# A weight-gradient stage that lands its loads in the place of WoT, starts them one step early, and walks its tiles downwards

## The chip, the cores and the metric

The kernel runs on one core of a Trainium2 chip. The metric is device time in microseconds (us); three runs of the kernel before gave 4724.1 to 4726.25, median 4724.49. One further execution was taken by the hardware profiler; every line of a profile below is from such an execution.

A core has five engines with their own instruction queues: PE (TensorE, matrix products; its weight loads are shown apart as PEld), DVE (VectorE), ACT (ScalarE), POOL (GpSimd) and SP (SyncE, which here only issues transfers). Transfers (DMAs) are issued on SP's, ACT's and POOL's queues.

## The reference

It is the backward pass of a block with a recurrent attention layer and a gated MLP, for 2048 tokens of width 640. The attention goes through the tokens in 64 segments of 32. Eight memory rows go ahead of each segment, and the first eight output rows are the memory of the next:

```
for s in range(n_seg):
    h = concatenate([mem, xs])              # 8 + 32 rows
    q, k, v = h @ Wq, h @ Wk, h @ Wv        # 32 heads of 128
    p = softmax(where(mask, q k^T * scale, -1e9))
    o = (p v) @ Wo
    mem = o[:8]; outs.append(o[8:])
```

The block returns `x + s * g`, where `s` is the attention of the normalised `x` and `g` a gated MLP of it. Asked for are the output and the gradients with respect to x, mem0, Wq, Wk, Wv, Wo, w1, w2 and w3, for a given `grad_out`. This document is about the point where the recurrence of the backward pass has ended and the gradients of Wq, Wk and Wv begin.

## The kernel before

The kernel goes through stages: MLP forward with the normalisation, the recurrence forward, the recurrence backward (`phase4_Abwd`), the gradients of the attention's projections (`phase6_Awgrads`), the gradient of Wo (`phase6b_gWo`) and the MLP backward (`phase5_Bbwd_ln`). In each of the stages of interest `in_order` fixes the instructions of each engine to the order in which the code writes them. Between two stages a scheduler may interleave, as long as buffers and data allow it. It also sets the semaphores: an instruction waits for whatever last used its buffer. A buffer is a range of the on-chip memory (SBUF); pools are stacked, and a later pool lies where an earlier one has been.

**The loop ahead.** `phase4_Abwd` runs `chain(t, gap)` for t from 63 down to 0 (L1184). Each step is one chain of dependent small products: the memory gradient times WoT (`packed_half`, L306), the gradients of v, k and q for eight rows, and the products of these with WvT, WkT and WqT (`packed_out`, L325), which `fold_add` sums into `fsum`. The next step needs that sum. In between, `gap` calls other work at named points (W0, W1, G1 to G6); in the last steps there is none left to call. The step's outputs go to device memory (HBM): rows of `GOS`, `DSR`, and, after the last step, the stores `out_dram<-fsum` by `fold_store`. The WoT matrix fills the tile tagged `w0` and WqT the one tagged `w1` of pool W0, 40 KB per partition each.

**The gradient stage.** The tokens are cut into 22 tiles (`NTL`): 20 of three segments with 96 tokens and 24 memory rows, then one with 96 and 24 and one with 32 and 8. The heads are cut into 8 quarters of four heads (the code calls a quarter `qd`). A unit is a pair of quarter and tile; 176 units are worked through, quarter by quarter, in the tile order 20, 21, 0, 1, ..., 19. For a unit,

- `ld(u)` (L1542) loads `dS` and `P` (120 x 512) and three row tiles `r` (g, q, k). SP issues five transfers and POOL three to six small ones for the memory rows (`load_m`, L245). There are five sets of buffers (`NB`).
- `s1` (L1563) transposes `dS` on PE, and DVE copies the result to `dST`.
- `s2` (L1573) forms three products (PE, L1578), which ACT and DVE copy out as gradient rows (`gr`, or `grs` for tiles 20 and 21, L1585 to L1589).
- `s3` (L1602) transposes these (PE, L1610), and ACT and DVE copy them into a ring (`ghacc`, at L92 and L90), which holds the last 384 tokens and a fixed piece of 128.
- `s4` (L1623) takes a block of 128 tokens from the ring, multiplies it by the quarter's weights `w` in twelve matmuls (L1628), and adds to `ghacc`, the running sum of the input gradient. The list `parts` says at which position in the quarter each half block is due.
- `wg` (L1642), at a quarter's end, multiplies the token rows `hr` by all gradient rows `gr` to give 512 columns of each weight gradient (PE, L1647).

The stage begins with `ld_to(3)`, `ld_w(0)` (three weights of 640 KB), `ld_to(5)` and `head(0)`, that is s1, s2 and s3 of the first two units. Then the loop at position p of a quarter loads unit p + 7, multiplies unit p + 2, transposes unit p + 3, turns unit p + 1 and does the s4 due. At units 6 to 11 SP also loads `hr`, 3.3 MB in all. The memory for all this is taken when pool W0 is already closed: first the sum and ring (pool `xw`), which lie where WoT and WqT were, and above them the stage's own buffers.

**Semaphores of transfers.** SP's transfers take eight semaphores in turn, POOL's another eight. A transfer waits for the one eight places before on its queue to have landed.

Of the kernel before, what the change touches and what calls it, by code (L numbers as in the profile page):

```python
# [9 lines left out]
BF16 = mybir.dt.bfloat16  # L10
# [6 lines left out]
P = 128  # L17
# [250 lines left out]
def turned_load(k, dst, src):  # L268

    k.nc.sync.dma_start_transpose(dst, src)  # L270
# [118 lines left out]
def phase3_Afwd(k, W0, W4, Wv, Wk_, out2):  # L389
    nc, tc = k.nc, k.tc  # L390
    D, DC, S, H, HD, T = k.D, k.DC, k.S, k.H, k.HD, k.T
    Wq = W4.tile([P, DC, HD], BF16, name="Wq", tag="w2")
    Wo = W4.tile([P, H, D], BF16, name="Wo", tag="w3")
    with tc.tile_pool(name="ast", bufs=1) as st:
        kTs = [st.tile([P, H, 120], BF16, name=f"kT{i}") for i in range(2)]

        vt = st.tile([P, HD // 2], BF16, name="vt")
        hxs = [st.tile([P, DC, 32], BF16, name=f"hx{i}") for i in range(2)]
        qTs = [st.tile([P, 4, P], BF16, name=f"xqT{i}") for i in range(3)]
        xPs = [st.tile([P, 4, P], BF16, name=f"xP{i}") for i in range(3)]  # L400
        PTs = [st.tile([P, 4, P], BF16, name=f"xPT{i}") for i in range(2)]
        oTm = st.tile([P, H, 32], BF16, name="oTm")
        first_part(k, Wv, Wk_, Wq, Wo, kTs, vt, hxs, qTs + xPs + PTs + [oTm])
        with tc.tile_pool(name="aps", bufs=1, space=bass.MemoryType.PSUM) as ps, \
                tc.tile_pool(name="apm", bufs=1, space=bass.MemoryType.PSUM) as psm:
            banks = [psm.tile([P, 512], F32, name=f"bank{i}") for i in range(3)]
            own = kTs, vt, hxs, qTs, xPs, PTs, oTm
            WT = recurrence(k, W0, W4, Wv, Wk_, Wq, Wo, own, ps, banks)
            phase4_Abwd(k, out2, W4, WT, own, ps, banks)


def first_part(k, Wv, Wk_, Wq, Wo, kTs, vt, hxs, rest):
# [667 lines left out]
        eng.dma_start(k.GX0[x0 - k.GB0:x0 - k.GB0 + w, cg * 1024:(cg + 1) * 1024], sg[0:w, :])  # L1080


def phase4_Abwd(k, out2, W4, WT, own, ps, banks):
    nc, tc = k.nc, k.tc
    D, DC, S, H, HD, T = k.D, k.DC, k.S, k.H, k.HD, k.T
    out2f = out2.flatten_outer_dims()
# [4 lines left out]
    for s in range(3):  # L1091
        t0 = (2, 0, 1)[s]
        n = (T - 1 - t0 + 2) // 3
# [10 lines left out]
    with tc.tile_pool(name="gst", bufs=1) as st, tc.tile_pool(name="gchain", bufs=1) as ch, \  # L1104
# [6 lines left out]
        four = lambda ap: ap.rearrange("p (i c) -> p i c", i=4)  # L1111
# [281 lines left out]
        def gap_of(t):  # L1393
            def at(f, tt, i0, i1=None):
                b = batch.get(tt, ())
                for u in b[i0:i0 + 1 if i1 is None else i1]:
                    f(*u)

            def gap(g):
                if g == "W0":  # L1400
                    ride_ld(t - 1)
                    at(turn, t, 0)
                elif g == "W1":
                    at(turn, t, 1)
                    at(gmem_ld, t + 1, 2)
                elif g == "G1":
                    at(dprob, t, 0)
                elif g == "G2":
                    at(dprob, t, 1)
                    at(turn, t, 2)  # L1410
                    at(dsoft, t, 0)
                elif g == "G3":
                    if t > 0:
                        load_xp(t - 1)
                    at(dsoft, t, 1)
                    at(gmem_ld, t, 0)
                elif g == "G4":
                    at(dprob, t, 2)
                elif g == "G5":
                    at(gmem_ld, t, 1)  # L1420
                elif g == "G6":
                    at(dsoft, t, 2)
                for i in range(WARM.get(g, 0)):
                    nc.tensor.matmul((bA if g in ("W1", "G2") else bB)[:], k.ident[:], WqT[:, 0, 0:512], start=True, stop=True)
            return gap
        todo = pro + todo

        def chain_consts():
            nc.gpsimd.memset(bdf, 0.0)
# [61 lines left out]
                nc.gpsimd.dma_start(*later.pop(0))  # L1491
        assert not later
        in_order(k, start)


def phase6_Awgrads(k, X, out0, out3, out4, out5):

    nc, tc = k.nc, k.tc
    D, DC, S, H, HD, T, NTL, NT = k.D, k.DC, k.S, k.H, k.HD, k.T, k.NTL, k.NT
# [5 lines left out]
    R = 384  # L1505
    NB = 5
    assert NS == 8 * NF and NW == NF and (96 * NF) % R == 0 and S - 96 * NF == P
    order = [NF, NF + 1] + list(range(NF))
    with tc.tile_pool(name="h6i", bufs=3) as io, tc.tile_pool(name="h6", bufs=1) as hp, \
            tc.tile_pool(name="h6g", bufs=1) as gp, tc.tile_pool(name="h6a", bufs=1, space=bass.MemoryType.PSUM) as pa:  # L1510
        start = len(nc.cur_bb.bb.instructions)
        hr = hp.tile([P, NF, D], BF16, name="hr")
        grs = [hp.tile([P, NF, 512], BF16, name=f"gr{i}") for i in range(3)]
        xt = X.tile([P, NT * D + 3 * 2 * (R + P)], F32, name="ghacc", tag="x")
        acc = xt[:, 0:NT * D].rearrange("p (w d) -> p w d", d=D)
        ring = xt[:, NT * D:].bitcast(BF16).rearrange("p (i j c) -> p i j c", i=3, j=4)
        dSs = [hp.tile([120, 4, P], BF16, name=f"dS6{i}") for i in range(NB)]
        dSTs = [hp.tile([120, 4, P], BF16, name=f"dST6{i}") for i in range(2)]
        Prs = [hp.tile([120, 4, P], BF16, name=f"P6{i}") for i in range(NB)]
        for i, tt in enumerate(dSTs):  # L1520
            (nc.gpsimd, nc.vector)[i % 2].memset(tt[:], 0.0)
        units = [(qd, tl) for qd in range(8) for tl in order]
        st, Ws, cnt = {}, {}, dict(w=0, s=0, g=0, l=0, x=0)

        def bank(kind, base, m):
            i = cnt[kind]
            cnt[kind] += 1
            return f"a{base + i % m}"

        def ld_w(qd):  # L1530
            c0 = qd * 512
            ws = []
            for i, src in enumerate((k.A_Wv, k.A_Wk, k.A_Wq)):
                w = gp.tile([P, 4, D], BF16, name="w6", tag=f"w6{i}")
                if i == 0 or qd == 0:
                    nc.sync.dma_start(w[:], k.WVT[:, 4 * qd:4 * qd + 4, :] if i == 0 else k.WQK[i - 1])
                else:
                    turned_load(k, w[:], src.rearrange("d h e -> d (h e)")[:, c0:c0 + 512])
                ws.append(w)
            Ws[qd] = ws  # L1540

        def ld(u):  # L1542
            qd, tl = units[u]
            c0, h0 = qd * 512, qd * 4
            ns, nm, nx, n = k.geo(tl)
            dS, Pr = dSs[u % NB], Prs[u % NB]
            nc.sync.dma_start(dS[0:n], k.DSR[tl][:, h0:h0 + 4, :])
            nc.sync.dma_start(Pr[0:n], k.PR[tl][:, h0:h0 + 4, :])
            rw = []
            for nm_ in ("g", "q", "k"):  # L1550
                r = io.tile([120, 512], BF16, name="r6", tag=f"r6{nm_}", bufs=NB)
                src = k.g_src(tl, c0, c0 + 512) if nm_ == "g" else k.x_src(tl, nm_, c0, c0 + 512)
                k.load_x(r, 0, src, nc.sync)
                k.load_m(r, tl, nm_, c0, c0 + 512, nc.gpsimd)
                rw.append(r)
            st["l", u] = (dS, Pr, rw)

        def ld_to(u):
            while cnt["l"] < min(u, len(units)):
                ld(cnt["l"])  # L1560
                cnt["l"] += 1

        def s1(u):  # L1563
            n = k.geo(units[u][1])[3]
# [48 lines left out]
        parts = [[] for _ in range(NTL)]  # L1613
        for h in range(2):
            parts[1 + h].append((NT - 1, R, h))
        for w in range(NT - 1):
            p = (P * (w + 1) - 1) // 96 + 2
            for h in range(2):
                parts[min(p + h, NTL - 1)].append((w, P * (w % 3), h))

# [57 lines left out]
            s1(u0 + 2)  # L1678
            yield

        ld_to(3)
        ld_w(0)
        ld_to(5)
        for _ in head(0):
            pass
# [507 lines left out]
@with_exitstack  # L2193
def kernel(
    ctx: ExitStack,
    tc: tile.TileContext,
    A_x: bass.AP,
    A_mem0: bass.AP,
    A_Wq: bass.AP,
    A_Wk: bass.AP,  # L2200
    A_Wv: bass.AP,
    A_Wo: bass.AP,
    A_seg_len,
    B_x: bass.AP,
    B_w1: bass.AP,
    B_w3: bass.AP,
    B_w2: bass.AP,
    grad_out: bass.AP,
    out_0: bass.AP,
    out_1: bass.AP,  # L2210
    out_2: bass.AP,
    out_3: bass.AP,
    out_4: bass.AP,
    out_5: bass.AP,
    out_6: bass.AP,
    out_7: bass.AP,
    out_8: bass.AP,
    out_9: bass.AP,
):
    outs = [out_0, out_1, out_2, out_3, out_4, out_5, out_6, out_7, out_8, out_9]  # L2220
    k = K(ctx, tc, A_x, A_mem0, A_Wq, A_Wk, A_Wv, A_Wo, B_w1, B_w3, B_w2, grad_out, outs)
    try:
        seg = int(A_seg_len)
    except Exception:
        seg = 32
    assert seg == k.SEG
    k.setup_consts()
    k.setup_dram()
    with tc.tile_pool(name="W0", bufs=1) as W0:
        Wv, Wk_ = [W0.tile([P, k.DC, k.HD], BF16, name=nm, tag=tag) for nm, tag in (("Wv", "w0"), ("Wk", "w1"))]  # L2230
        phase12_ln_Bfwd(k, Wv, Wk_)
        with tc.tile_pool(name="W4", bufs=1) as W4:
            phase3_Afwd(k, W0, W4, Wv, Wk_, out_2)
    with tc.tile_pool(name="xw", bufs=1) as X:
        wo_ops = phase6_Awgrads(k, X, out_0, out_3, out_4, out_5)
        phase5_Bbwd_ln(k, X, *wo_ops, out_1, out_6, out_7, out_8, out_9)


# [33 lines left out]
```

## Time and profile before

| | |
|---|---|
| median of three runs | 4724.49 us |
| profiled execution, its time | 4722.13 us |
| profiled execution, span from first to last instruction | 4720.1 us |
| PE busy | 4476.3 us, 95% |
| DVE, ACT, POOL busy | 48%, 34%, 44% |
| granted TensorE clock, mean | 0.985 |

| stretch (us from the start) | what runs | PE busy | DMA share |
|---|---|---|---|
| 1830 to 2905 | backward recurrence, steps up to t = 1 | 1021.8 of 1075 | 0.71 |
| 2905 to 2920 | its last step | 13.6 of 15 | 0.12 |
| 2920 to 2942 | first units of the gradient stage | 10.5 of 22 | 0.83 |
| 2942 to 2985 | units on | 43.0 of 43 | 1.00 |
| 2985 to 3005 | units on, with loads of `hr` | 13.7 of 20 | 0.98 |
| 3005 to 3030 | the first quarter's end | 24.9 of 25 | 0.67 |
| 3030 to 4147 | gradient of weights, quarters 2 to 8 | 1108.8 of 1117 | 0.48 |
| 4147 to 4720 | gradient of Wo and MLP backward | 548.2 of 573 | 0.75 |

A row of the profile names a line of the kernel, an engine, and the tiles written and read (`t<-ident,dS`: tile t from ident and dS). "DMA share" is the mean busy share of the core's 16 transfer engines; in short windows it can come out a little over 1. A wait is put down to what ended it last.

### The profile page before, as it was taken

The page shows a single profiled execution, that of the slowest core. Times are in us where ns is not written, and L with a number is a line of the kernel's source. Part 1 is how long each engine was busy: PE and PEld are TensorE (multiplying, and loading weights), DVE is VectorE, ACT ScalarE, POOL GpSimd, SP SyncE. Part 2 cuts the span into 40 slices and gives each one's busy share as a digit, 9 for nine tenths or more (in the row PEclk, how much of TensorE's full clock was granted, in tenths as well). Part 3 has the DMA queues.
Part 4 walks back from the last instruction along what each step waited for, and adds up shares of the span by engine and source line. Part 5 has one row for each costly group of instructions (what it writes and reads, how often), then busy time and mean ns, then how long its engine had stood idle before and what let it go on. Part 6 is the DMA issues. An engine that isn't in the chain of part 4 may idle for free. (4 is left out here: it accounts for less than half of the span.)

```text
span 4720.1 us, 160254 instructions
## 1 busy us (share of the span) xinstructions
PE 4476.3 (95%) x64504; PEld 2824.1 (60%) x64504; DVE 2244.0 (48%) x7156; ACT 1588.8 (34%) x4360; POOL 2093.8 (44%) x3514
## 2 busy tenths in 40 slices
PE   8998999999999888999999998999999999999999
PEld 4544555555555555666666665666567666666675
DVE  8734666666666534555555553343234332311460
ACT  5432555555544533333333332232223322200000
POOL 6522555555555423444444444454345533311340
PEclk9998999999999998999999998999999999999999
DMA  8773666666555678777777774754345543579673
GB/s 265 238 244 106 176 182 179 177 180 178 175 174 167 169 179 230 208 215 203 212 210 213 205 210 133 163 150 133 109 125 157 145 125 109 170 219 208 154 183 100
DMA packets 977976, 834.81 MB, mean 177 GB/s; under 512 B 518674, under 2 KB 859862, under 8 KB 975272
## 3 DMA queue, kind: packets, MB, share of 16 engines
q1 hardware_dynamic: 765871, 549.75, 42.5%
q0 software_dynamic: 129088, 226.29, 16.2%
q10 hardware_dynamic: 82275, 48.52, 4.0%
q8 instruction: 509, 8.34, 0.8%
q14 instruction: 233, 1.91, 0.2%
HBM read 472.66 MB, written 310.33 MB: 166 GB/s over the span
## 5 line engine op out<-in xcount | busy, mean ns | idle before, releaser
L1647 PE MATMUL wg<-gr,hr 128*128 128x512 bf16 x2400 | 521.7, 379 | 0.0
L1628 PE MATMUL g<-w,ghacc 128*128 128x320 bf16 x3072 | 460.3, 300 | 0.8
L1647 PEld LDWEIGHTS <-hr 128*128 128x128 bf16 x2400 | 234.1, 98 | 278.7
L306 PEld LDWEIGHTS <-hx 128*32 128x32 bf16 x10240 | 247.0, 96 | 233.8 <-issue 19.6
L1628 PEld LDWEIGHTS <-ghacc 128*128 128x128 bf16 x3072 | 288.7, 98 | 104.6 <-ACT ghacc L92 2.2
L90 DVE CAST wgo<-wg 128x512 bf16<-128x512 f32 x72 | 49.8, 692 | 471.2 <-PE wg L1647 471.2
L90 DVE CAST stg<-bank 128x512 bf16<-128x512 f32 x256 | 177.0, 692 | 164.0 <-PE bank L306 152.6
L880 POOL DMA_DIRECT2D OR<-xv x163 | 89.8, 551 | 361.0 <-ACT xv L92 334.7
L92 ACT COPY ghacc<-t6g 128x768 bf16<-128x768 bf16 (+1 forms) x176 | 137.2, 780 | 303.6 <-PE t6g L1610 302.6
L1593 POOL DMA_DIRECT2D GSP<-grs x48 | 25.7, 549 | 474.3 <-ACT grs L1585 473.2
L325 PEld LDWEIGHTS <-gkv 128*8 128x8 bf16 x8192 | 178.6, 87 | 83.6 <-issue 4.1
L1324 POOL DMA_DIRECT2D VTD<-gvT x176 | 129.8, 743 | 218.0 <-ACT gvT L1323 210.2
L812 ACT ACTIVATE xP<-xsp,xnm 120x120 bf16<-120x120 f32 (+1 forms) x540 | 186.6, 374 | 29.2 <-DVE xnm L794 29.2
L832 POOL TENSOR_TENSOR xP<-xP,xrz 120x480 bf16<-120x480 bf16 x163 | 161.3, 989 | 76.3 <-DVE xrz L831 47.0
L336 DVE TENSOR_TENSOR fsum<-bank,fup 64x160 bf16<-64x160 f32 x254 | 69.5, 311 | 261.4 <-ACT fup L334 258.8
L1634 DVE TENSOR_TENSOR ghacc<-ghacc,g 128x320 f32<-128x320 f32 x192 | 93.5, 487 | 209.4 <-PE g L1628 209.4
L92 ACT CAST wgo<-wg 128x512 bf16<-128x512 f32 x48 | 28.1, 586 | 479.8 <-PE wg L1647 406.9
L1371 POOL DMA_DIRECT2D GXP<-gks x157 | 91.5, 583 | 195.2 <-ACT gks L1369 193.0
L325 PE MATMUL bank<-Wo,oTm 128*32 128x320 bf16 x4032 | 154.6, 307 | 18.5 <-DVE oTm L684 18.5
L325 PE MATMUL bank<-WvT,gkv 128*8 128x320 bf16 x4096 | 170.2, 310 | 0.0
L306 PE MATMUL bank<-Wq,hx 128*32 128x512 bf16 x2560 | 163.0, 384 | 5.4 <-DVE stg L90 5.4
L325 PE MATMUL bank<-WkT,gkv 128*8 128x320 bf16 x4096 | 162.8, 299 | 4.2 <-issue 2.5
(390 smaller groups left out, 10944.1 us busy)
## 6 DMA issues: line engine op xcount, KB each, us to landing
QVS<-stg SPq DMA_DIRECT2D x128, 256.0 KB
kT<-VTD SPq DMA_DIRECT2D x64, 320.0 KB
PR<-xP POOLq DMA_DIRECT2D x168, 120.0 KB, 3.3
VTD<-gvT POOLq DMA_DIRECT2D x168, 120.0 KB, 4.1
dS<-DSR SPq DMA_DIRECT2D x168, 120.0 KB
P<-PR SPq DMA_DIRECT2D x168, 120.0 KB
OR<-xv POOLq DMA_DIRECT2D x163, 120.0 KB, 3.1
orr<-OR SPq DMA_DIRECT2D x14, 1280.0 KB
```

Source lines behind the costliest of these rows:

```text
L90: return nc.vector.tensor_copy(out, in_)
L92: return nc.scalar.copy(out, in_)
L306: k.nc.tensor.matmul(bank[32 * g:32 * g + 32, :], x[:, dc, :], W[:, dc, c0:c0 + 512], start=(dc == 0), stop=(dc == k.DC - 1), tile_positio ...
L325: k.nc.tensor.matmul(pm[p0:p0 + nq, 0:320], x[:, h, :], W[:, h, 320 * b:320 * b + 320], start=(first and i == 0), stop=(last and i == 15), ...
L812: nc.scalar.activation(Pb[0:n, j, 0:n], sp[0:n, j, :], ACT.Exp, bias=nmx[0:n, j:j + 1], scale=k.scale, accum_out=Z[0:n, j:j + 1])
L832: eng.tensor_tensor(Pb[0:n, :, 0:n], Pb[0:n, :, 0:n], bc_last(rz[0:n], n), ALU.mult)
L880: q.dma_start(k.OR[120 * tl:120 * tl + n, c0:c0 + 512], v[0:n])
L1324: nc.gpsimd.dma_start(k.VTD[tl][:, :, h0:h0 + 4, :], vTq[:])
L1371: (nc.sync if (tl, qd) in pro else nc.gpsimd).dma_start(k.GXP[tl, :, qd, 0:ns], ks[:].rearrange("p s i h m -> p s i (h m)"))
L1628: nc.tensor.matmul(pg[:], ring[:, i, j, r0:r0 + P], Ws[qd][i][:, j, 320 * h:320 * h + 320], start=(i == 0 and j == 0), stop=(i == 2 and j ...
L1634: nc.vector.tensor_tensor(a, a, pg[:], ALU.add)
L1647: nc.tensor.matmul(pw[:], hr[:, tl, dc * P:(dc + 1) * P], grs[i][:, tl, :], start=(tl == 0), stop=(tl == NF - 1))
```

## The change

It has four parts, all at this border.

1. The landing buffers (five sets of `dS`, `P` and three `r`, and the three weights) become parts of one tile `land` in pool W0 under the tag `w0`, that is in the place of WoT. Two of the gradient row buffers (`gr01`) go to tag `w1`, the place of WqT. The pool stays open until the stage has ended.
2. A class `Fetch` holds the load functions, so that the last step of the loop can call them: units 0 and 1 at gap G1, unit 2 at G2, the weights at G3. The stage itself starts with `ld_to(5)`.
3. The tile order becomes 20, 21, 19, 18, ..., 0, and `parts` follows it.
4. The sum and its ring (`xw`) are allocated from the right end of the memory.

```
+                if t == 0 and g == "G1":
+                    fetch.append(Fetch(k, W0))
+                if t == 0 and g in ("G1", "G2"):
+                    fetch[0].to(2 if g == "G1" else 3)
+                if t == 0 and g == "G3":
+                    fetch[0].w(0)
...
+class Fetch:
+
+    def __init__(self, k, W0):
+        self.k, self.NB = k, 5
+        NF = k.NTL - 2
+        self.units = [(qd, tl) for qd in range(8) for tl in [NF, NF + 1] + list(range(NF - 1, -1, -1))]
+        self.st, self.Ws, self.n = {}, {}, 0
+        t = W0.tile([P, 5 * self.NB * 512 + 12 * k.D], BF16, name="land", tag="w0")
+        four = lambda ap: ap.rearrange("p (h c) -> p h c", h=4)
+        b = [[t[0:120, 512 * (5 * i + j):512 * (5 * i + j) + 512] for i in range(self.NB)] for j in range(5)]
+        self.dS, self.P = [[four(x) for x in y] for y in b[0:2]]
+        self.rows = dict(zip("gqk", b[2:5]))
+        c = 5 * self.NB * 512
+        self.ws = [four(t[:, c + 4 * k.D * i:c + 4 * k.D * (i + 1)]) for i in range(3)]
+
+    def w(self, qd):
+        k, nc = self.k, self.k.nc
+        for i, src in enumerate((k.A_Wv, k.A_Wk, k.A_Wq)):
+            if i == 0 or qd == 0:
+                nc.sync.dma_start(self.ws[i], k.WVT[:, 4 * qd:4 * qd + 4, :] if i == 0 else k.WQK[i - 1])
+            else:
+                turned_load(k, self.ws[i], src.rearrange("d h e -> d (h e)")[:, 512 * qd:512 * qd + 512])
+        self.Ws[qd] = self.ws
+
+    def ld(self, u):
+        k, nc = self.k, self.k.nc
+        qd, tl = self.units[u]
+        c0, h0 = qd * 512, qd * 4
+        n = k.geo(tl)[3]
+        dS, Pr = self.dS[u % self.NB], self.P[u % self.NB]
+        nc.sync.dma_start(dS[0:n], k.DSR[tl][:, h0:h0 + 4, :])
+        nc.sync.dma_start(Pr[0:n], k.PR[tl][:, h0:h0 + 4, :])
+        rw = []
+        for nm in ("g", "q", "k"):
+            r = self.rows[nm][u % self.NB]
+            src = k.g_src(tl, c0, c0 + 512) if nm == "g" else k.x_src(tl, nm, c0, c0 + 512)
+            k.load_x(r, 0, src, nc.sync)
+            k.load_m(r, tl, nm, c0, c0 + 512, nc.gpsimd)
+            rw.append(r)
+        self.st["l", u] = (dS, Pr, rw)
...
-    order = [NF, NF + 1] + list(range(NF))
+    st, Ws, cnt = fetch.st, fetch.Ws, dict(w=0, s=0, g=0, x=0)
+    units, ld_to, ld_w = fetch.units, fetch.to, fetch.w
...
-        grs = [hp.tile([P, NF, 512], BF16, name=f"gr{i}") for i in range(3)]
+        grt = W0.tile([P, 2, NF, 512], BF16, name="gr01", tag="w1")
+        grs = [grt[:, 0], grt[:, 1], hp.tile([P, NF, 512], BF16, name="gr2")[:]]
...
-        for w in range(NT - 1):
-            p = (P * (w + 1) - 1) // 96 + 2
+        for w in range(NT - 2, -1, -1):
+            p = NF + 1 - P * w // 96
             for h in range(2):
                 parts[min(p + h, NTL - 1)].append((w, P * (w % 3), h))
...
-        ld_to(3)
-        ld_w(0)
         ld_to(5)
         for _ in head(0):
...
-    with tc.tile_pool(name="W0", bufs=1) as W0:
+    with ExitStack() as ws, ExitStack() as xs:
+        W0 = ws.enter_context(tc.tile_pool(name="W0", bufs=1))
...
-    with tc.tile_pool(name="xw", bufs=1) as X:
-        wo_ops = phase6_Awgrads(k, X, out_0, out_3, out_4, out_5)
+        X = xs.enter_context(tc.tile_pool(name="xw", bufs=1, side="right"))
+        wo_ops = phase6_Awgrads(k, X, W0, fetch, out_0, out_3, out_4, out_5)
+        ws.close()
         phase5_Bbwd_ln(k, X, *wo_ops, out_1, out_6, out_7, out_8, out_9)
```

More of the change, by code (lines that the diff above doesn't have):

```diff
@@ L408, in phase3_Afwd @@
             WT = recurrence(k, W0, W4, Wv, Wk_, Wq, Wo, own, ps, banks)
-            phase4_Abwd(k, out2, W4, WT, own, ps, banks)
+            return phase4_Abwd(k, out2, W0, W4, WT, own, ps, banks)
 def first_part(k, Wv, Wk_, Wq, Wo, kTs, vt, hxs, rest):
@@ L1080, in gx_block, with phase4_Abwd @@
         eng.dma_start(k.GX0[x0 - k.GB0:x0 - k.GB0 + w, cg * 1024:(cg + 1) * 1024], sg[0:w, :])
-def phase4_Abwd(k, out2, W4, WT, own, ps, banks):
+def phase4_Abwd(k, out2, W0, W4, WT, own, ps, banks):
     nc, tc = k.nc, k.tc
@@ L1426, in phase4_Abwd @@
         todo = pro + todo
+        fetch = []
         def chain_consts():
@@ L1493, in phase4_Abwd, with to, phase6_Awgrads @@
         in_order(k, start)
-def phase6_Awgrads(k, X, out0, out3, out4, out5):
+    return fetch[0]
+class Fetch:
[35 more added lines that the diff above has]
+        self.st["l", u] = (dS, Pr, rw)
+    def to(self, u):
+        while self.n < min(u, len(self.units)):
+            self.ld(self.n)
+            self.n += 1
+def phase6_Awgrads(k, X, W0, fetch, out0, out3, out4, out5):
     nc, tc = k.nc, k.tc
@@ L1516, in phase6_Awgrads @@
         ring = xt[:, NT * D:].bitcast(BF16).rearrange("p (i j c) -> p i j c", i=3, j=4)
-        dSs = [hp.tile([120, 4, P], BF16, name=f"dS6{i}") for i in range(NB)]
         dSTs = [hp.tile([120, 4, P], BF16, name=f"dST6{i}") for i in range(2)]
-        Prs = [hp.tile([120, 4, P], BF16, name=f"P6{i}") for i in range(NB)]
         for i, tt in enumerate(dSTs):
             (nc.gpsimd, nc.vector)[i % 2].memset(tt[:], 0.0)
-        units = [(qd, tl) for qd in range(8) for tl in order]
-        st, Ws, cnt = {}, {}, dict(w=0, s=0, g=0, l=0, x=0)
         def bank(kind, base, m):
@@ L1528, in bank @@
             return f"a{base + i % m}"
[L1530 to L1561, printed above, removed]
         def s1(u):
@@ L2232 @@
         with tc.tile_pool(name="W4", bufs=1) as W4:
-            phase3_Afwd(k, W0, W4, Wv, Wk_, out_2)
-    with tc.tile_pool(name="xw", bufs=1) as X:
-        wo_ops = phase6_Awgrads(k, X, out_0, out_3, out_4, out_5)
+            fetch = phase3_Afwd(k, W0, W4, Wv, Wk_, out_2)
+        X = xs.enter_context(tc.tile_pool(name="xw", bufs=1, side="right"))
+        wo_ops = phase6_Awgrads(k, X, W0, fetch, out_0, out_3, out_4, out_5)
+        ws.close()
         phase5_Bbwd_ln(k, X, *wo_ops, out_1, out_6, out_7, out_8, out_9)
```

## The prediction

> **What bounds the kernel now.** I read the page first, then windows by stage, then the waits of TensorE between 2920 and 3010 us, then the timelines of PE, SP and POOL there. The page says that TensorE is the bound and nearly full, so only its gaps can be won:
>
> ```profile
> PE 4476.3 (95%) x64504; PEld 2824.1 (60%) x64504; DVE 2244.0 (48%) x7156; ACT 1588.8 (34%) x4360; POOL 2093.8 (44%) x3514
> ```
>
> The windows place the gaps beside the change. Columns: stretch, its length, PE, PEld, DVE, ACT, POOL busy us, granted clock, DMA share, GB/s.
>
> ```profile
> 2910.00:2915.00 5.00, 4.83 (x87) 2.52 (x86) 2.04 (x8) 0.45 (x2) 1.31 (x2) 0.66 0.02 1
> 2930.00:2935.00 5.00, 0.02 (x1) 0.00 (x0) 0.69 (x1) 0.22 (x1) 2.18 (x5) 0.50 1.05 335
> 2995.00:3000.00 5.00, 2.49 (x31) 1.86 (x28) 1.03 (x3) 1.88 (x3) 1.42 (x3) 1.00 1.10 113
> ```
>
> In the loop's last step (2905 to 2920.65) the transfer engines are idle; 15 us later TensorE is idle and they are full; and at 2995 the same again. The waits of PE from 2920 to 3010, by what ended them (us in total, times, longest):
>
> ```profile
> PE t L1568 <- DMA dS<-DSR: 11.9, 5, 8.3
> PE r6p L1578 <- DMA r<-QVS: 2.5, 1, 2.5
> PE r6p L1578 <- DMA r<-GOS: 1.2, 1, 1.2
> ```
>
> All are loads of units. The timeline of PE shows the two places; in brackets is the idle time ahead and what ended it:
>
> ```profile
> 2922.00 0.37 PE L1568 MATMUL t<-ident,dS 120*128 120x120 bf16 x4 [1.35 <-DMA dS<-DSR]
> ...
> 2938.29 0.58 PE L1568 MATMUL t<-ident,dS 120*128 120x120 bf16 x4 [8.27 <-DMA dS<-DSR]
> ...
> 2941.11 3.32 PE L1628 MATMUL g<-w,ghacc 128*128 128x320 bf16 x12
> ...
> 2945.66 1.79 PE L1628 MATMUL g<-w,ghacc 128*128 128x320 bf16 x12
> ...
> 3000.71 0.40 PE L1578 MATMUL r6p<-r,dS 120*128 120x128 bf16 x4 [2.48 <-DMA r<-QVS]
> ...
> 3002.28 3.41 PE L1628 MATMUL g<-w,ghacc 128*128 128x320 bf16 x12
> ```
>
> The first is unit 3's `dS`, queued behind 1.9 MB of weights. The second, 2987 to 3002, is six waits of 0.98, 0.79, 0.36, 0.74, 2.48 and 0.94, 6.3 us together, while the `hr` loads share the queues. After each gap twelve matmuls take 3.3 to 3.4 us instead of 1.79. From 3030 to 4147 TensorE is busy 1108.8 of 1117 us, so a gain made ahead of it is kept.
>
> **What the Trainium skill says.** "DMA: Bandwidth & Descriptors", section "Issuing engines are not separate DMA queues": transfers started by SP and POOL run on the same 16 engines and interleave. The trace agrees: while the weights are in flight, POOL's row loads of 16 KB take 7.3 us and those of 8 KB 5.2 (medians, 2920 to 2945), and POOL's `out_dram<-fsum`, issued ahead of the weights, took 2.3. "TensorE: Matmul & The Clock Gate", section "What's actually happening": the clock is halved after an idle window of about 3.4 us and restored after a busy one. It agrees: 0.50 at 2925 to 2940, full from 2945.
>
> **The change part by part.** The profiled execution is 4722.1 us (span 4720.1); the median of the runs is 2.4 above, and I subtract from both alike.
>
> *Loads moved into the last step.* SP now issues there 15 loads of units 0 to 2, the weights' 3, and, as the order of the built program shows, unit 3's `dS` and `P` even ahead of them: 20 at 0.31 to 0.42 us, about 7.5 us. They wait for the last matmul that reads WoT, which ends at 2907.4, so units 0 to 2 are issued by about 2914.5. Queued behind them on SP: the GOS store (0.4 us later; the `fup` copy that waits for it is due only at 2920.4), and the DSR stores (2913.4 to 2914.5; their reader, tile 0, is now last in the quarter). The weights follow at 2915.3 instead of 2926.65. POOL issues 9 row loads at 0.57, 2907.5 to 2912.6, ahead of its DSR stores, due at 2913.66 anyway. So the moves cost nothing in the step: the queues idle there (DMA share 0.02), and its TensorE chain waits for none of these. Without that cover it would be the 7.5 us of SP.
>
> *What they remove.* Transposing unit 0 starts at 2921.4 rather than 2922.0, because its PSUM bank is held until `fsum` is formed at 2921.38: 0.55 us. Waits of 1.22 and 0.71 us for rows vanish. Unit 1's products then end at about 2926.1 instead of 2928.6, 2.5 us earlier. The 8.27 us cannot recur for the same reason: unit 3's `dS` lands by about 2911.
>
> *What is late next.* The new layout puts the sum and its ring at the right end of memory, where the ring now covers `fsum`. In the built program the first copies into the ring, on ACT and DVE, wait for the two stores `out_dram<-fsum`. On POOL these stand behind the fill of `dST` (which still ends at 2918.8, waiting for WkT's last matmuls) and eight row loads, to 2923.4; and each reuses a semaphore of the load eight places before, so it waits for that load to land, amid the weights: 2919.4 + 5.2 to 7.8, the middle 2925.6. (7.8: POOL's issue at 2938.07 waited for a load of 2930.2.) The store itself took 2.3 in the quiet and small loads 5.2 in the press: +3.7. So the ring opens at about 2929.3 (between 2926.9 and 2934.5). Behind the ring copy stand, on ACT, 0.80, then the copy of unit 1's product, 0.58, which frees the bank for unit 2's; DVE has the same. TensorE is then 2.3 us from unit 3's transposes, and from there 2.8 to the first s4, as in 2938.29 to 2941.11. So s4 starts at 2929.3 + 5.1 = 2934.4 instead of 2941.1: **6.7 us** (ends 9.1 and 1.5). The weights, 1.97 MB from 2915.5 at some 230 GB/s, are in by about 2925 and don't hold it.
>
> *The loads' lead.* Before, unit 7's first load is issued at 2944.89; now its buffer is free when unit 2's second product is done, about 2931.7. That is 13.2 us earlier, with TensorE 6.7 earlier, so 6.5 more lead. By bytes: until 2927.5 the windows show 1.7 MB moved; the new order could move about 4.6, and 2.9 MB at 235 GB/s are 12.3 us, less some 2 us without an open request: 3.6 more lead. I take 4.7 of the 6.3 us, **4.7 us**; ends 0 and 6.3. Of the 1.6 us lost to the half clock at 3002 I take **0.8**.
>
> *The rest.* Descending tiles: TensorE, DVE and ACT have the same kinds of instruction in the same places, counted in the built program, the s4 of a block still follows its last tile by the same number of steps, and loads are of the same size. Nothing, -1 to +1. One tile for landing: the row waits between SP and POOL loads of a buffer are fewer, and lie five units back: nothing. The stage after: its first loads still wait for the last gradient matmuls, which overlap them in both layouts; hidden by the 22 us that pass before its second quarter of rows is needed. Nothing, -1 to +1.
>
> Sum: 6.7 + 4.7 + 0.8 = 12.2; 4722.1 becomes 4709.9, and the median 4724.5 becomes **4712.3**.
>
> **Rivals.** (1) The lead does not carry: 2942 to 2985 runs at DMA share 1.00, and if what counts there is bytes against time, the stall at 3000 stays and only the head is won, 4724.5 - 6.7 = 4717.8. Against: the latency between issue and use there is 6 us, with five buffers that allow more. (2) All is bound by transfer to the quarter's last unit, and the early bytes are lost again to a fuller queue: 4723. For it: share 0.9 or more nearly to 3022. Against: TensorE runs without a gap from 2942 to 2985 and after 3005. (3) The new wait is short, the ring opens at 2926 and all 6.3 us come back with the clock: 10 + 6.3 + 1.6 = 18, 4706.5. (4) Slower: the wait for `out_dram<-fsum` replaces the old one and is longer. Each us of it beyond 2936.0 delays the first s4 past today's; with the 5.5 us of lead and clock on the other side, it costs over 0.2% (9.4 us) only from an opening at 2951, some 25 us after the stores' issue: say 2952, 4735. Nothing of POOL in the trace took over 7.8. (5) That the loads are not moved at all is excluded by the built order.
>
> **How the numbers follow.** Likeliest, with its sizes: 4708.5 to 4716, chance 0.55. Rival 1: 0.20. Rival 2: 0.11. Rival 3: 0.09. Rival 4: 0.05. The bound of 0.2% (about what a measurement of this kernel can tell) lies at 4715.0: faster takes 0.53 of the first and rival 3, 0.62; same takes the rest of the first and rivals 1 and 2, 0.33; slower 0.05. The range, 4707 to 4720.5, holds the first two whole and half of rival 3, and leaves out the rest.
>
> **What would show it.** Right: DMA share over 0.8 from 2910 to 2925; no wait for `dS` of 8 us; ACT's first ring copy idle for several us, ended by `out_dram<-fsum`, and TensorE idle there, some 3 to 6 us around 2926 to 2931; the first s4 at about 2934; the waits at 2985 to 3005 smaller than 2 us together; the stage from 3030 on merely shifted. Wrong: a last step longer than 15.6 us (SP or POOL in the way), a ring that opens after 2936, waits for `dS` at quarter starts above today's 5.2 us, or gaps past 4147 that were not there.

## The result, and the profile after

The changed kernel took 4710.39 us (median of 22 runs, 4697.55 to 4722.58), the kernel before 4724.51 (median of 22, 4707.42 to 4732.95). The ratio is 0.9971, with a 95% interval of 0.9961 to 0.9981: 13.7 us less, between 9.0 and 18.4; the lower end is just short of the 0.2% (9.4 us) that the prediction took as its bound. The profiled execution took 4716.74 us, with a span of 4715.0.

Single executions of one kernel differ by some 10 us either way, and a good part of that arises in the 2900 us ahead of the change: the last step's product with WoT started between 2903.3 and 2917.7 us in the runs below, with hardly a changed instruction before it. So times are counted in what follows **from the start of that product**, called 0: before, that is 2905.11; after, 2911.35.

| Counted from 0 (us) | before | after | gain |
|---|---|---|---|
| first `t` of unit 0 | 16.89 | 16.66 | 0.2 |
| ring's first copy on ACT | 21.87 | 26.69 | -4.8 |
| first product into `g` (s4) | 36.00 | 31.66 | 4.3 |
| first product into `wg` (end of the first quarter) | 125.30 | 117.14 | 8.2 |
| start of the Wo gradient (`oa`) | 1242.18 | 1231.71 | 10.5 |
| end of the span | 1814.99 | 1803.65 | 11.3 |

The page's first line of the changed kernel. It has as many instructions as before, and TensorE is as full as it was:

```profile
PE 4485.5 (95%) x64504; PEld 2828.0 (60%) x64504; DVE 2243.0 (48%) x7156; ACT 1587.0 (34%) x4360; POOL 2090.2 (44%) x3514
```

Windows of the changed kernel, columns as in the prediction (stretch, length, PE, PEld, DVE, ACT, POOL busy us, granted clock, DMA share, GB/s). The transfer engines now work in the last step, TensorE still stands at 2931 to 2936, and the second stall has moved to 3010:

```profile
2916.00:2921.00 5.00, 5.00 (x87) 2.62 (x86) 1.75 (x7) 0.36 (x1) 4.22 (x8) 0.66 0.74 225
2931.00:2936.00 5.00, 1.13 (x10) 0.78 (x9) 0.00 (x0) 0.00 (x0) 2.21 (x4) 0.50 1.04 287
3010.00:3015.00 5.00, 3.12 (x20) 2.16 (x21) 1.96 (x5) 0.59 (x1) 4.25 (x8) 0.74 0.55 154
```

What PE waited for from 2925 to 3016 (us in total, times, longest). The 11.9 us for `dS` are gone; one wait of 7.2 us for ACT stands in their place:

```profile
PE r6p L1598 <- ACT grs L1605: 7.2, 1, 7.2
PE r6p L1598 <- DMA land<-QVS: 2.4, 2, 1.9
PE r6p L1598 <- DMA land<-DSR: 1.0, 1, 1.0
```

The timeline of PE at both places, the idle time ahead and what ended it in brackets. The first block of twelve s4 matmuls takes 2.35 us where it took 3.32, and at 3012.94 it is still slow, at half clock:

```profile
2928.01 0.37 PE L1588 MATMUL t<-ident,land 120*128 120x120 bf16 x4 [0.88 <-DVE fsum L336]
...
2939.37 1.01 PE L1598 MATMUL r6p<-land 120*128 120x128 bf16 x8 [7.23 <-ACT grs L1605]
...
2943.01 2.35 PE L1648 MATMUL g<-land,ghacc 128*128 128x320 bf16 x12
...
3011.38 0.38 PE L1598 MATMUL r6p<-land 120*128 120x128 bf16 x4 [1.93 <-DMA land<-QVS]
3012.26 0.48 PE L1598 MATMUL r6p<-land 120*128 120x128 bf16 x4 [0.50 <-DMA land<-QVS]
...
3012.94 3.21 PE L1648 MATMUL g<-land,ghacc 128*128 128x320 bf16 x12
```

Behind the 7.23 us stands ACT, whose first copy into the ring waited 8.08 us. The timeline of ACT names a load as what ended it; in the built program that copy waits for both stores `out_dram<-fsum` and the last step's stores into `DSR`, and for none of the loads into `land`, and the landing of `out_dram<-fsum` fits the time:

```profile
2938.04 0.80 ACT L92 COPY ghacc<-t6g 128x768 bf16<-128x768 bf16 x1 [8.08 <-DMA land<-QVS]
```

POOL's timeline has the stores' issue, and the list of transfers their time from issue to landing (last column, us):

```profile
2929.58 1.02 POOL L343 DMA_DIRECT2D out_dram<-fsum  x2
```

```profile
out_dram<-fsum POOLq DMA_DIRECT2D x2, 5.0 KB, 7.6
```

The same line of the kernel before:

```profile
out_dram<-fsum POOLq DMA_DIRECT2D x2, 5.0 KB, 2.3
```

The timeline of SP after shows it held at unit 2's `P` for 1.69 us, and the weights leaving at 14.0:

```profile
2920.92 1.69 SPq L1535 DMA_DIRECT2D land<-PR  x1
...
2925.34 0.46 SPq L1523 DMA_DIRECT2D land<-WVT  x1
2925.84 1.95 SPq L1523 DMA_DIRECT2D land<-WQK  x2
```

From the first `wg` to the Wo gradient the changed kernel needs 1114.6 us instead of 1116.9. The waits of PE there, before and then after:

```profile
PE t L1568 <- DMA dS<-DSR: 5.2, 7, 1.4
```

```profile
PE t L1588 <- DMA land<-DSR: 2.9, 6, 0.7
```

### The profile page after: what moved, and what is told of

Its sections match the earlier page's. It is cut to its first block, busy times and chain, and to the rows that moved or that the text cites. A ratio compares the mean times of both kernels' runs of the same rounds, so it can differ in the third digit from the quotient of the medians.

```text
span 4715.0 us, 159806 instructions
## 1 busy us (share of the span) xinstructions
PE 4485.5 (95%) x64504; PEld 2828.0 (60%) x64504; DVE 2243.0 (48%) x7156; ACT 1587.0 (34%) x4360; POOL 2090.2 (44%) x3514
## 5 line engine op out<-in xcount | busy, mean ns | idle before, releaser
L1648 PE MATMUL g<-land,ghacc 128*128 128x320 bf16 x3072 | 459.3, 300 | 0.8
```

Source lines behind the costliest of these rows:

```text
L1648: nc.tensor.matmul(pg[:], ring[:, i, j, r0:r0 + P], Ws[qd][i][:, j, 320 * h:320 * h + 320], start=(i == 0 and j == 0), stop=(i == 2 and j ...
```

## The experiments

All marks of all runs in one table, in us from 0, and the sum of PE's waits between s4 and `wg`, which is the second stall. Each row is one profiled execution; e9, g1 and h1 were timed as well.

| Run | ring | first s4 | first `wg` | s4 to `wg` | of it PE waits | Wo gradient | end |
|---|---|---|---|---|---|---|---|
| before | 21.87 | 36.00 | 125.30 | 89.30 | 6.3 | 1242.2 | 1815.0 |
| after | 26.69 | 31.66 | 117.14 | 85.48 | 3.7 | 1231.7 | 1803.7 |
| e1_clear_store | 25.90 | 30.86 | 120.30 | 89.44 | 7.1 | 1235.6 | 1810.9 |
| e2_no_early | 27.33 | 32.30 | 120.01 | 87.71 | 5.6 | 1234.3 | 1805.0 |
| e3_weights_late | 25.45 | 30.42 | 116.15 | 85.73 | 3.5 | 1230.9 | 1804.2 |
| e6_weights_first | 23.45 | 28.41 | 115.85 | 87.44 | 6.3 | 1231.1 | 1803.4 |
| f1_store_act | 23.41 | 28.38 | 118.96 | 90.58 | 6.5 | 1233.2 | 1807.8 |
| f2_no_store | 18.60 | 24.29 | 114.37 | 90.08 | 7.9 | 1231.1 | 1808.8 |
| f3_gated | 21.77 | 33.40 | 125.61 | 92.21 | 7.8 | 1240.7 | 1815.5 |
| e5_after_no_hr | 25.80 | 30.77 | 110.54 | 79.77 | 0 | 1225.4 | 1802.4 |
| e7_hr_spread | 25.83 | 30.80 | 110.48 | 79.68 | 0 | 1226.1 | 1793.7 |
| e9_ascending | 25.70 | 30.67 | 118.61 | 87.94 | 4.7 | 1233.2 | 1807.2 |
| g1_own_spread | 18.71 | 25.00 | 110.48 | 85.48 | 2.4 | 1226.3 | 1796.1 |
| h1_own_spread_wide | 18.41 | 24.93 | 109.74 | 84.81 | 2.0 | 1223.8 | 1794.9 |

My theory going in: the stores of `fsum` hold the ring and with it the first s4; what is gained ahead is kept as far as the loads' lead reaches. The first rival: the weights would hold the first s4 in any case.

**e1, the store's tile moved.**

```diff
-            fs = fold_add(k, pm, ch, "gstg")
+            fs0 = fl.tile([64, 320], BF16, name="fsum0", tag="gks", bufs=2) if t == 0 else None
+            fs = fold_add(k, pm, ch, "gstg", fs0)
```

> The sum of the last step's Gkm fold (`fsum`) lies in a tile below the range that `ghacc` and its ring take, so the ring's first copies no longer wait for `out_dram<-fsum`; nothing else differs from the changed kernel. All marks are counted from the start of the last step's product with WoT. Changed kernel: ring's first copy ends its wait at 26.7, first product into `g` at 31.66, first product into `wg` at 117.1. Theory A (the store's landing alone holds the ring): the ring's copy goes as soon as unit 0's products are there, about 21 to 22, and the first `g` product comes 4 to 5 us earlier, at 26.5 to 27.5; what is gained there is kept at `wg` only as far as the loads allow. Theory B (the weights, issued at 14.0 to 16.4 on SP, land at about 30 and the first `g` product needs them anyway): the wait moves from ACT's copy to the products, whose idle time then ends with a landing of WVT or WQK, and the first `g` product comes at 30 to 31.5.

Neither came. The tile now lies above the ring's bytes, but in the built program the ring's first copies still wait for both stores, which took 7.3 us here: the edit did not do what it says. So the run is the changed kernel a second time, with the same waits, and that makes it useful. Two executions of the same work differ by 0.8 us at the first s4, 3.2 at `wg`, 3.9 at the Wo gradient and 7.2 at the end. Differences of that size are not read as effects below.

**e2, no loads inside the last step.**

```diff
-                if t == 0 and g == "G1":
-                    fetch.append(Fetch(k, W0))
-                if t == 0 and g in ("G1", "G2"):
-                    fetch[0].to(2 if g == "G1" else 3)
-                if t == 0 and g == "G3":
-                    fetch[0].w(0)
...
+        ld_to(3)
+        ld_w(0)
         ld_to(5)
```

> The changed kernel's buffers, ring and descending order, but no load inside the last step: units 0 to 2, the weights and units 3 and 4 are issued where the kernel before issues them, at the start of the stage. If the early loads are the whole of the gain (theory A), the marks go back to those of before: first `g` product at 36 to 37 (before 36.0, changed 31.66), first `wg` product at 124 to 126 (125.3 and 117.1). Rival: the freed buffers and the order do part of it (the loads need wait for nothing of the pool of before): then the first `g` product comes at 33 to 35 without any early load.

Neither number: the first s4 came at 32.30. The timeline of SP says why; it begins at 2.39, as in the changed kernel (2.38), and not at 13.12 as before:

```profile
2914.31 0.33 SPq L1528 DMA_DIRECT2D land<-DSR  x1
```

SP's order in the built program is not that of the text: since the landing buffers are free from the last matmul with WoT on, SP's loads start there whether the loop's last step asks for them or not. Those of unit 0 and most of unit 1 go ahead of the step's last stores (8.28), those of unit 2 right behind them. Only POOL's row loads come later (13.7 instead of 2.65), and PE waits 3.55 us for one of them, in the shadow of the ring. So the place of the code in the loop shows as 2.6 us at the Wo gradient, less than the 3.9 by which two executions of one kernel differ.

**f3, the buffers free late.** To make the loads late for certain, one small DVE copy into every landing buffer waits for the last step's `gqT`; the rest is e2.

```diff
+                if t == 0 and g == "G3":
+                    fetch.append(Fetch(k, W0))
+                    nc.vector.tensor_copy(fetch[0].all[:, 0:40 * 512:512],
+                                          k.gate[:].rearrange("p h e -> p (h e)")[:, 0:40])
```

> The changed kernel's buffers, layout and order, units 0 to 2 and the weights asked for at the stage's start, and every landing buffer first written by one small DVE copy that needs the last step's `gqT` (done at 11.9): no load of the stage can be issued before about 12.2, as in the kernel before (13.1), where the buffers came free only then. In the run without early loads SP issued units 0 to 2 ahead of their place all the same, from 2.4 on, since the buffers were free. If the early issue on SP, which the buffers' new place allows, is the whole gain (theory A): first `g` product at 35 to 38, first `wg` at 123 to 127, as before (36.0 and 125.3). If the layout and the descending order do the rest by themselves: first `g` product at 31 to 33, `wg` at 119 to 121, as in the run without early loads (32.3 and 120.0).

The loads start at 11.9, in SP's timeline:

```profile
2919.10 0.33 SPq L1533 DMA_DIRECT2D land<-DSR  x1
```

The first `wg` at 125.61, the Wo gradient at 1240.7 and the end at 1815.5 are those of the kernel before (125.30, 1242.2, 1815.0). The first s4, at 33.40, lies between the two expectations. The old wait is back, in PE's timeline at unit 3's `dS`, behind the weights:

```profile
2937.75 0.58 PE L1587 MATMUL t<-ident,land 120*128 120x120 bf16 x4 [6.48 <-DMA land<-DSR]
```

So the early start of SP's loads, which the buffers' place allows, carries the gain: 6.4 us at the Wo gradient between f3 and e2, and 5.2 to 9.8 between f3 and each of after, e1, e2, e3 and e9, whose loads start early. Past the first s4 the layout and the order by themselves bring nothing that these marks can tell.

**e3 and e6, the weights later and sooner.** e3 takes `fetch[0].w(0)` out of the last step and puts `ld_w(0)` at the stage's start; e6 has e1's edit and asks for the weights in G1, after unit 1:

```diff
-                if t == 0 and g == "G3":
+                if t == 0 and g == "G1":
                     fetch[0].w(0)
```

> The changed kernel with units 0 to 2 in the last step, but the weights issued at the start of the stage, after unit 2 and before unit 3. Theory A: SP is held back in the last step by the loads ahead of the weights, so that their place in the program hardly counts: they are issued at 14 to 18 as in the changed kernel (14.0 to 16.4), and the first `g` product stays within 1 us of 31.66. Rival: the place counts, the weights are issued 3 us or more later, and the first `g` product comes at 34 to 36.

> As the run with the cleared store, and besides the weights are issued after units 0 and 1 and ahead of unit 2. Theory A (the store was the only wait): same first `g` product as with the cleared store alone, within 1 us. Theory B (weights in flight hold the first `g` product once the store is out of the way): 2 to 4 us earlier than with the cleared store alone; unit 2's first product may then wait 1 to 2 us for its DSR.

e3: 30.42, sooner than the changed kernel's two executions by 1.2 and 0.4 us, so the place in the program hardly counts, though not for the reason given: SP sent WVT first of all, at 2.4, and the other two at 14.5. e6: SP's weights left at 8.9 to 11.4, ahead of the stores by some 9 us or more. The stores were issued later than in e1 (20.3 against 18.0), and still the ring opened at 23.45 and the first s4 came at 28.41, both some 2.4 us sooner. Their line in the list of transfers, in e1 and then in e6:

```profile
out_dram<-fsum POOLq DMA_DIRECT2D x2, 5.0 KB, 7.3
```

```profile
out_dram<-fsum POOLq DMA_DIRECT2D x2, 5.0 KB, 2.3
```

What the weights hold up is thus the store. The first s4 follows the ring by 4.96 to 4.97 us in after, e1, e2, e3 and e6 alike, so theory B, as put, has the right cause in the wrong place.

**f2, without the store, and f1, with it on ACT.** f2 leaves out the two last stores; f1 issues them from ACT.

```diff
-            fold_store(nc.gpsimd, k.m_rows(k.GWO, t - 1) if t > 0 else out2f, fs)
+            fold_store(nc.gpsimd if t > 0 else nc.scalar, k.m_rows(k.GWO, t - 1) if t > 0 else out2f, fs)
```

> The changed kernel without the last step's two stores of `fsum` to out_dram (8 x 320 each; those rows of the output stay unwritten), so that the ring's first copies have nothing of that kind to wait for. In the changed kernel and in the four runs so far the first product into `g` came 4.96 to 4.97 after the ring's first copy on ACT (opened at 26.7, 25.9, 27.3, 25.5 and 23.5 from the start of the last step's product with WoT). Theory A (the store's landing alone holds the ring, and the ring the first `g` product): the ring's copy comes at 19 to 20, right behind unit 0's products, and the first `g` product at 24 to 26.5. Theory B (the weights' 1.97 MB are in the way of it all): the ring's copy comes early, but the products of unit 1 or the first `g` product then wait for a landing, and the first `g` product stays at 28 to 31.

> The changed kernel with those two stores issued by ACT's queue instead of POOL's, behind the copy into `fup` and ahead of unit 0's cast. Theory A': what makes them slow is POOL's queue (6 row loads ahead of them in it), and on ACT's they land within 2 to 3 us of the issue at about 16.5: ring at 19 to 20.5, first `g` product at 24 to 26.5. Theory B': any small store is slow while SP's 1.97 MB of weights are in flight on the same DMA engines: it lands at 23 to 26, the ring opens then, and the first `g` product comes at 28 to 31.

f2 is theory A: ACT's copy goes without any wait, and the first s4 comes at 24.29. The stores into `DSR`, for which the copy waits too, are still there (as they are in g1 and h1 below, with the ring at 18.7 and 18.4), so they don't hold it. The timelines of ACT and PE in f2:

```profile
2929.22 0.80 ACT L92 COPY ghacc<-t6g 128x768 bf16<-128x768 bf16 x1
```

```profile
2934.91 2.50 PE L1649 MATMUL g<-land,ghacc 128*128 128x320 bf16 x12
```

But of 7.4 us gained there on the changed kernel's profile, 2.8 are left at `wg` and 0.6 at the Wo gradient (of 6.6 on e1's, 5.9 and 4.5). The second stall is 7.9 us long in f2, against 3.7 in the changed kernel's profile but 7.1 in e1, so that one execution doesn't tell whether the earlier start has lengthened it. The longest waits of PE in f2 between s4 and `wg`; for the first the profile shows no cause:

```profile
PE r6p L1599 <- issue: 3.7, 1, 3.7
PE r6p L1599 <- DMA land<-QVS: 2.8, 3, 1.0
PE r6p L1599 <- ACT gr L1610: 1.2, 1, 1.2
```

f1 is B': it is not POOL's queue. On ACT the stores are issued at 16.3, and the ring opens 7.1 us later, at 23.4. The timeline of ACT in f1:

```profile
2934.03 0.64 ACTq L343 DMA_DIRECT2D out_dram<-fsum  x2
...
2941.11 0.80 ACT L92 COPY ghacc<-t6g 128x768 bf16<-128x768 bf16 x1 [5.01 <-DMA land<-GOS]
```

This is what the Trainium skill says in "DMA: Bandwidth & Descriptors", section "Issuing engines are not separate DMA queues": another issuing engine saves the issue and not the transfer.

**e5 and e7, the bytes of `hr`.** e5 leaves the loads of `hr` out (3.3 MB, not the 2.6 of its expectation) and sets `hr` to zero on DVE instead; e7 cuts them in halves over twice as many units:

```diff
-                if 6 <= u < 11:
-                    c = 4 * (u - 6)
+                if 6 <= u < 16:
+                    c = 2 * (u - 6)
...
-                if u == 11:
+                if u == 16:
```

> The changed kernel with the loads of `hr` (2.6 MB, eleven transfers at units 6 to 11) left out; `hr` is set to zero on DVE in ten pieces at units 6 to 15, so that the gradients of Wq, Wk and Wv are computed from zeros. If those bytes are what the units' loads fall behind in the second stall: no idle time of PE of more than 0.5 us between the first `g` product and the first `wg` product apart from the half clock, `wg` 80 to 82.5 after `g` (changed kernel 85.5; other runs of the same layout 85.7 to 89.4; before 89.3). Rival: the stall is the late start of the loads and stays, 84 or more.

> The changed kernel with the loads of `hr` cut into twenty transfers over units 6 to 15 (two tiles each) and the rest at unit 16, in place of ten over units 6 to 10 and the rest at unit 11. Bytes, order of the units and the ring's wait stay. Theory (the second stall comes where five units' loads and five large pieces of `hr` ask for more than the DMA engines move; half of that per unit stays below it): first `g` product at 30 to 32 as before, no stall above 1 us between 60 and 110, first `wg` 80 to 82.5 after the first `g`, at 111 to 114 (changed kernel 117.1, without `hr` 110.5). Rival (the quarter as a whole moves all that the DMA engines can, so that the stall is only put off to units 12 to 16): `wg` stays 85 or more after `g`.

Both as the theory has it, a little under its 80 us. Without `hr`, s4 to `wg` takes 79.77 us; with `hr` spread, 79.68, with all its bytes moved. The whole list of waits of PE in e7, from unit 0 to the first `wg`:

```profile
PE r6p L1598 <- ACT grs L1605: 7.2, 1, 7.2
PE t L1588 <- DVE fsum L336: 1.2, 1, 1.2
```

Windows of e5 and of e7 in the middle of the quarter. With `hr` the transfer engines are full at some 240 GB/s; without it the units ask for 189:

```profile
2950.00:3000.00 50.00, 50.00 (x594) 40.83 (x592) 31.48 (x71) 23.84 (x39) 42.88 (x77) 1.00 0.70 189
```

```profile
2960.00:2995.00 35.00, 35.00 (x418) 28.62 (x417) 17.62 (x41) 16.59 (x28) 25.78 (x46) 1.00 1.02 236
```

e5 and e7 are one execution each, but both lie 5.7 us below the shortest quarter of the runs that load `hr` over five units (85.48). So the second stall is shown to come from `hr`'s bytes coming in a lump: they overdraw the transfers, the units' lead is used up, and PE waits.

**g1 and h1, both gaps taken at once.** g1 is e7, with the last `fsum` in the first columns of `gr01`, where no wait of the ring reaches; h1 spreads `hr` further.

```diff
-            fs = fold_add(k, pm, ch, "gstg")
+            fs = fold_add(k, pm, ch, "gstg", k.grt[0:64, 0, 0, 0:320] if t == 0 else None)
...
+                    k.grt = W0.tile([P, 2, k.NTL - 2, 512], BF16, name="gr01", tag="w1")
```

> As the run with `hr` spread, and the last step's `fsum` is put into the first columns of `gr01` (row tile 0's place, written last), which is no freed buffer: the store to out_dram stays, and nothing of the ring waits for it. Theory: ring at 18.6 and first `g` product at 24 to 25 as in the run without the store, and this time kept, since the second stall is gone: first `wg` product at 104 to 107, start of the Wo gradient at 1217 to 1222 (changed kernel 1231.7, before 1242.2), and a time 8 to 14 us below the changed kernel's: ratio to the kernel before 0.9942 to 0.9955. Rival (bytes set the quarter's end): what the ring gains is lost again by `wg`, which comes at 110 to 114, and the ratio is 0.996 to 0.997.

> As the run with `fsum` in `gr01`'s place, with the ten pieces of `hr` at units 2, 3, 5, 7, 8, 10, 12, 13, 15 and 17 and the rest at unit 18, in place of units 6 to 15 and 16. With `hr` over units 6 to 15 both runs reached the first `wg` product at 110.48, whether the ring opened at 25.8 or at 18.7, and the run without `hr` at 110.54; in the run with the ring at 18.7 the DMA share was 0.97 to 1.11 from 45 to 90, against 0.81 to 0.85 from 24 to 45. Theory (what is lost there is the rate that the DMA engines reach in those units, and the first units have room for part of it): no idle time of PE above 1 us between 70 and 105, first `wg` at 105 to 108, start of the Wo gradient at 1220 to 1224, ratio to the kernel before 0.9945 to 0.9970. Rival (all the quarter's bytes together set its end): `wg` at 110 to 113 again, ratio 0.9955 to 0.9980.

In both the ring opened at 18.4 to 18.7 and the first s4 came at 25, as expected; and in both `wg` came where e7 has it, at 110. That is the rival's number; its cause, the bytes, is borne out in part only. The window of g1's middle shows 50 us of full transfers:

```profile
2945.00:2995.00 50.00, 50.00 (x599) 40.96 (x597) 27.05 (x61) 22.88 (x38) 38.56 (x70) 1.00 1.02 240
```

Behind it PE waits again. Its waits from there to `wg`, in g1 and then in h1:

```profile
PE r6p L1600 <- DVE eo_g L1685: 1.2, 1, 1.2
PE r6p L1600 <- DMA land<-QVS: 1.2, 2, 0.9
```

```profile
PE r6p L1600 <- DMA land<-DSR: 1.5, 1, 1.5
PE r6p L1600 <- DMA land<-QVS: 0.5, 1, 0.5
```

e7 runs the quarter without a wait, 79.7 us after its first s4. g1 starts 5.8 us sooner and needs 5.8 more: 2.4 are these waits, and the rest is TensorE at half clock, at the start and after the waits. So less than half of the loss can be put down to transfers; and as no run has an early ring without `hr`, what the rest would be with fewer bytes is open. The windows of g1 show it (e7 has 0.86 in its first 6 us and 1.00 from there on):

```profile
2929.00:2935.00 6.00, 6.00 (x46) 4.56 (x44) 1.69 (x4) 1.52 (x3) 4.90 (x9) 0.51 0.85 252
...
3000.00:3005.00 5.00, 4.76 (x40) 3.27 (x39) 1.75 (x5) 1.58 (x3) 2.78 (x6) 0.69 0.63 146
```

Timed, g1 took 4703.60 us (median of 6), ratio to the kernel before 0.9964 (0.9951 to 0.9978), and h1 4705.00 (median of 5), ratio 0.9963 (0.9950 to 0.9977). Both beat the kernel before; against the changed kernel's 0.9971 the intervals overlap, so that step is not settled by time, though their Wo gradient starts 5.4 and 7.9 us sooner than in the changed kernel's profile. e7 was run once, 4698.72 us.

**e9, the tiles in ascending order, and unit 2 asked for one gap later.**

```diff
-                if t == 0 and g in ("G1", "G2"):
+                if t == 0 and g in ("G1", "G3"):
...
-        self.units = [(qd, tl) for qd in range(8) for tl in [NF, NF + 1] + list(range(NF - 1, -1, -1))]
+        self.units = [(qd, tl) for qd in range(8) for tl in [NF, NF + 1] + list(range(NF))]
...
-        for w in range(NT - 2, -1, -1):
-            p = NF + 1 - P * w // 96
+        for w in range(NT - 1):
+            p = (P * (w + 1) - 1) // 96 + 2
```

> The changed kernel with the tiles of every quarter in ascending order again (20, 21, 0, 1, ...), the parts of `s4` in their order of before, and unit 2 (tile 0, whose DSR rows the last step itself stores) asked for after those stores. Theory (the order is worth nothing by itself): first `g` product within 2 us of 31.66, first `wg` within 3 us of 117.1, ratio to the kernel before 0.9960 to 0.9982. Rival (the order is needed, since tile 0 waits for the last step's stores): unit 2's product waits, first `g` at 34 or later, ratio 0.998 or more.

The marks are the theory's, and between those of the changed kernel and e1 throughout. The time is not: 4716.22 us (median of 20), ratio 0.9987 (0.9980 to 0.9994), slower than expected and at the edge of the changed kernel's interval. The two ratios are 0.0016 apart, 7.6 us; an estimate from their two intervals, taken as independent, puts the difference between 2 and 13 us. So by time the order, or unit 2's place, seems worth something, up to half of the whole gain. But the two were timed on separate occasions, each against its own runs of the kernel before, and no stage of the profile shows a loss, so the cause stays open. g1 was timed beside e9, and is 12.6 us below it.

## Why the prediction was right, and where it was not

The time predicted was 4712.3, the time measured 4710.4, and faster was the likeliest outcome. The parts of the sum were less good than the sum: the two largest came out smaller than forecast, and what made up for them was not foreseen. That the total fits is in part luck.

- **The moves cost nothing in the last step: right.** Its last matmul starts at 15.39 instead of 15.15, and the step ends at 15.78, a little over the 15.6 named as a sign of being wrong; but PE waited for no transfer in it, and the difference lies in the last 44 products with WvT, which took 2.57 us instead of 2.31. SP was not done as early as worked out: units 0 to 2 were issued by 12.6 instead of 9.4, the weights at 14.0 instead of 10.2. Its waits show 1.0 us for the landing of an earlier `dS`, and the issue of unit 2's `P` took 1.69; the working had counted SP's issue times alone. The share of over 0.8 claimed for that time was 0.74, 0.45 and 0.80 in its three windows.
- **What gives the gain: the right event, put down to the wrong edit.** The step "loads moved into the last step" works by the buffers' place: e2 without the move keeps the first s4 at 32.3, f3 with the buffers late has lost all of it at `wg`.
- **First s4 6.7 us earlier: 4.3.** The mis-sized term is the ring. Predicted to open at 2929.3, which is 24.2 from 0, it opened at 26.69. The store was issued earlier than assumed (18.2, not 20.5) and took 7.6 us, not 3.7. TensorE's wait there, forecast at 3 to 6 us, was 7.2. From ring to s4 5.1 us were predicted, and 4.97 measured. That the weights don't hold the s4 was right (f2: 24.29), but they hold the store.
- **The lead 4.7 us and the clock 0.8: 3.8 together in the profile shown, and 2.0 in the mean of five.** Unit 7's first load left at 30.7 instead of 39.8: 9.0 us sooner, where 13.2 were forecast. The waits of the second stall, forecast below 2 us together, were 3.7. The five runs of this layout with `hr` and the store's issue as they were (after, e1, e2, e3, e9) need 85.5 to 89.4 from s4 to `wg`, 87.3 in the mean, against 89.3 in the one profile before: 2.0 us, within what two executions differ by. The half clock stayed (3.21 us at 3012.94).
- **The weak step is the sum itself.** It adds the head's gain to the lead's as if they were apart. Where `hr` is spread they are not: g1's ring opens 7.1 us sooner than e7's, and both reach `wg` at 110.48: what the head gains is paid for in half clock and in waits. With `hr` in its lump it is not settled, as f2's 2.8 of 7.4 and 5.9 of 6.6 us show. Rivals 1 and 2 had a part of it, bytes against time; but it is `hr`'s lump that counts, which e7 takes away without moving a byte less.
- **From 3030 on "merely shifted": 2.3 us better.** Waits for `dS` at quarter starts fell from 5.2 to 2.9 us; twelve of the thirteen profiles of the new layout have 1114.0 to 1115.9 us for that stretch, e9 with ascending tiles among them, and f2 1116.7, against 1116.9. This was not foreseen; its cause was not tested, and only one profile of the kernel before stands against them.
- **The clock in the kernel before: half right.** The prediction reads it as bearing out the idle window. It did come back 6 us into the work that follows the 8.27 us gap, as the prediction says. But it had fallen between 2923 and 2924, 6 us ahead of that gap, behind waits of 1.35 and 1.22 us:

```profile
2923.00:2924.00 1.00, 0.41 (x4) 0.33 (x5) 0.00 (x0) 0.00 (x0) 1.00 (x3) 0.86 0.52 150
2924.00:2925.00 1.00, 0.65 (x5) 0.42 (x4) 0.00 (x0) 0.00 (x0) 1.00 (x3) 0.50 0.37 109
```

- **Descending order, nothing:** by the marks yes; by the time perhaps some us, of open cause (e9). **Rivals 3 and 4** are out: the ring opened at 26.69, neither at 20.9 (their 2926) nor anywhere near 45.9 (2951).

The gain by marks is 11.3 us at the end of the span in the profile shown, 4.1 in e1, and 8.8 in the mean of the five runs; by time it is 13.7 (9.0 to 18.4). The marks of single executions cannot place more than that.

## What to carry to other kernels

Ask where a load's buffer comes free before asking where its call stands: here the queue ran ahead of the text by itself once the memory allowed it. A gap closed ahead of a stretch with full transfers is worth only what that stretch lets through, so look for the next stall and its bytes, and spread a lump of loads before opening anything sooner. And a small store that others wait for should leave ahead of the big loads, not close behind them.

## What was not expected of the hardware

- **A store of 5 KB took 2.3 to 2.9 us where the weights were sent later or 9 us and more ahead of it (before, f3, e6), 5.7 us where they were sent 7 to 8 us ahead (e2), and 6.3 to 7.6 us where two or all three of them were sent within 5 us ahead of it (after, e1, e3, e5, e7, e9).** The Trainium skill, "DMA: Bandwidth & Descriptors", section "Latency and other measured facts", puts a transfer's fixed cost at about 2 us, smaller under lighter load: the quiet case agrees, and the loaded one is three times that.
- **The clock fell to half without a long gap.** "TensorE: Matmul & The Clock Gate", section "What's actually happening", has it halved after an idle window of about 3.4 us. In f2 the only gap is 1.20 us, and less in truth: a matmul of 0.39 us that other traces show there (L1430 in after) isn't listed, only its weight load. Small products at 0.82 to 0.95 busy follow, and the clock still falls within 2929 to 2930 and stays at half for 7 us. Windows of one us in f2:

```profile
2926.00:2927.00 1.00, 0.00 (x0) 0.00 (x0) 0.52 (x2) 0.42 (x1) 1.00 (x3) 1.00 0.99 410
2928.00:2929.00 1.00, 0.90 (x16) 0.76 (x16) 0.95 (x3) 0.90 (x2) 0.76 (x2) 1.00 1.06 428
2929.00:2930.00 1.00, 0.95 (x14) 0.74 (x11) 0.36 (x1) 0.91 (x2) 0.00 (x0) 0.76 0.97 309
2930.00:2931.00 1.00, 1.00 (x11) 0.80 (x10) 0.48 (x1) 0.65 (x3) 0.00 (x0) 0.50 1.15 274
```
